# Batch 1's k' transposed by DMA with its projection one slot sooner, and the last output tile in three parts

## The chip, the cores and the metric

The kernel runs on one core of a Trainium2 chip. The metric is the time of one execution in microseconds (us), as the device reports it; lower is better. "Span" is the time from the first to the last instruction in a profiled execution; the reported time of the same execution is 1.7 to 1.8 us longer.

## The reference

Two parts, one behind the other. Linformer attention projects k and v along the sequence, so that scores are taken against 64 projected rows. Then comes a feed-forward network (FFN) with a quick GELU.

```python
k_proj = einsum('ks,bhsd->bhkd', E, k)          # E, F: 64 x 1024
v_proj = einsum('ks,bhsd->bhkd', F, v)          # 8 batches, 8 heads, 1024 rows, 64 wide
scores = (1/8) * q @ k_proj^T
attn   = softmax(scores)
x      = (attn @ v_proj)  -> 8192 tokens x 512
h      = x @ w_in                               # 512 x 2048
out    = (h * sigmoid(1.702 h)) @ w_out         # 2048 x 512
```

## The kernel before

The FFN works on 16 blocks of 512 tokens. In a block, 16 groups of four matmuls ("slots" 0 to 15) make `h`; then eight parts of eight matmuls (slots O = 16 and up) make the output, two parts for each of four output tiles. Attention for later blocks is put into those slots with `at(block, slot, work)`, so that TensorE never stands still. The parts that matter here:

```python
ps_f = ctx.enter_context(tc.tile_pool(name="ps_f", bufs=4, space=PSUM))   # f_tile: four buffers in rotation
...
def proj(b):                                   # k' and v' of batch b, 16 matmuls
    def go():
        kvps[b] = f_tile([P, H, D])
        ...
def k_tr(b, k_b, p0):                          # k' transposed on TensorE
    t_ps = f_tile([P, n, KP], BF16)
    for p in range(n):
        nc.tensor.transpose(t_ps[:, p, :], ..., ident[:KP, :KP])
    nc.vector.tensor_copy(kts[b % 2][:, p0:p0 + n, :], t_ps)
...
def kv_out(b):
    def go():
        ps = kvps.pop(b)
        k_b = att.tile([KP, H, D], BF16, name="k_b")
        nc.vector.tensor_copy(k_b, ps[LO])     # "the cast of k'"
        if b > 1:                              # batches 2 to 7: k' transposed by DMA
            nc.sync.dma_start_transpose(out=kts[b % 2], in_=k_b.rearrange("k h d -> k (h d)"))
        v_out(b, ps)
        kbs[b] = k_b
    return go
...
# the last output tile: two halves of 256 columns
for i, cp in enumerate((nc.scalar.copy, nc.vector.tensor_copy)):
    ms = slice(i * DM // 2, (i + 1) * DM // 2)
    l_ps = f_tile([P, DM // 2])
    for fc in range(FC):
        nc.tensor.matmul(l_ps, gts[j][:, fc, n * P:(n + 1) * P], w_out_sb[:, fc, ms], ...)
    cp(osb[j][:, n, ms], l_ps)
    nc.sync.dma_start(out=ov[:, c * JB + n, ms], in_=osb[j][:, n, ms])
...
at(1, 10, proj(1))
at(1, 11, kv_out(1))
at(1, 13, lambda: k_tr(1, kbs[1], 0))
at(1, 1, q_dma(1, 0, JB), q_dma(1, JB, JB))    # q of batch 1 transposed by DMA, same queue
for u in range(2):
    at(1, O, scores(2, u, None, u > 0))        # the first scores of batch 1: need k' of batch 1
...
load(j // NB2 + 2)                             # GpSimd's loads, two batches ahead: k, q, v for batch 2
```

There is one `k_sb` and one `v_sb` buffer (`bufs=1`). The load of batch b+1's k can therefore start only when the projection of batch b has read its own k. The projection sets free a 1 MB load.

The softmax here doesn't subtract the row's maximum and nothing guards it: scores larger than these inputs give would overflow.

Of the kernel before, what the change touches and what calls it, by code (L numbers as in the profile page):

```python
# [17 lines left out]
def kernel(ctx, tc, q, k, v, E, F,  # L18
                                                     moe_w_in, moe_w_out, out):
    nc = tc.nc  # L20
    B, H, S, D = q.shape
    KP, _ = E.shape
    DM, DFF = moe_w_in.shape
    P = 128
# [87 lines left out]
    kts = [consts.tile([P, HP, KP], BF16, name=f"kt{i}") for i in range(2)]  # L112
# [25 lines left out]
    def f_tile(shape, dt=F32):  # L138
        return ps_f.tile(shape, dt, name="f_ps")

    def warm(n):
        w_ps = ps_x.tile([P, TB], F32, name="x_ps")
        for _ in range(n):
            nc.tensor.matmul(w_ps, zeros[:, :P], zeros, start=True, stop=True)  # L144
# [6 lines left out]
    for i, cp in enumerate((nc.vector.tensor_copy, nc.scalar.copy)):  # L151
        t_ps = f_tile([P, J // 2, 2 * KP], BF16)
# [10 lines left out]
    def eft(j, cols=slice(0, 2 * KP)):  # L163
        return efts[j // (J // 2)][:, j % (J // 2), cols]


    kvps, kbs, qT, expT, xT, rbc, rdens = {}, {}, {}, {}, {}, {}, {}

    def proj(b):
        def go():  # L170
            kvps[b] = f_tile([P, H, D])
            for j in range(J):
                for e, r in enumerate((LO, HI)):
                    nc.tensor.matmul(kvps[b][r], eft(j, slice(e * KP, (e + 1) * KP)),  # L174
                                     (kt, vt)[e][b][:, :, j, :],
                                     start=(j == 0), stop=(j == J - 1))
        return go

    def proj0(e, h0, n):
        ps = f_tile([P, n, D])  # L180
        for j in range(J):
            nc.tensor.matmul(ps, ffs[:, j].rearrange("s i k -> s (i k)") if e else eft(j), (kt, vt)[e][0][:, h0:h0 + n, j, :],
                             start=(j == 0), stop=(j == J - 1))
        return ps

    def k_piece(h0, n):
        k_ps = proj0(0, h0, n)
        k_b = att.tile([KP, n, D], BF16, name=f"k0_b{h0}", bufs=1)
        nc.vector.tensor_copy(k_b, k_ps[LO])
        warm(2)  # L190
        k_tr(0, k_b, h0 // 2)

    def k_tr(b, k_b, p0):
        n = k_b.shape[1] // 2
        t_ps = f_tile([P, n, KP], BF16)
        for p in range(n):
            nc.tensor.transpose(t_ps[:, p, :], k_b[:, 2 * p:2 * p + 2, :].rearrange("k t d -> k (t d)"),
                                ident[:KP, :KP])
        nc.vector.tensor_copy(kts[b % 2][:, p0:p0 + n, :], t_ps)

    def vx_of(b, p):
        if b == 1:
# [13 lines left out]
    def v_out(b, v_ps):  # L216
        vv = v_ps[HI].rearrange("k (u x) d -> k u x d", x=4)
        for r, xs_ in ((LO, X_LO), (HI, X_HI)):
            if b == 1:
                vx = vx1[r, :, :D].rearrange("k (u x) d -> k u x d", x=4)  # L220
                nc.vector.tensor_copy(vx[:, :, xs_], vv[:, :, xs_])
            nc.vector.tensor_copy(vqs[b % 2][r].rearrange("k (u e) d -> k u e d", e=2), vv[:, :, xs_, :])

    def kv_out(b):
        def go():
            ps = kvps.pop(b)
            k_b = att.tile([KP, H, D], BF16, name="k_b")
            nc.vector.tensor_copy(k_b, ps[LO])  # L228
            if b > 1:
                nc.sync.dma_start_transpose(out=kts[b % 2], in_=k_b.rearrange("k h d -> k (h d)"))  # L230
            v_out(b, ps)
            kbs[b] = k_b
        return go

    q0s = [[consts.tile([P, 2, 2, P], BF16, name=f"q0T{g}{u}") for u in range(2)] for g in range(2)]
# [21 lines left out]
    def q_dma(b, j0=0, n=J):  # L257
        def go():
            if j0 == 0:
                qT[b] = att.tile([P, J, HP, P], BF16, name="qT")  # L260
            nc.sync.dma_start_transpose(out=qT[b][:, j0:j0 + n].rearrange("r j p s -> r (j p) s"),
                                        in_=qt[b][:, j0:j0 + n].rearrange("s j h d -> s (j h d)"))
        return go
# [102 lines left out]
    def x_tr(h, p, half):  # L366
        def go():
            x_sb = xs.pop((h, p, half)).rearrange("s (i t) d -> s i (t d)", i=2)
            n_ps = ps_x.tile([P, 2, P], BF16, name="x_ps")
            for i in range(2):  # L370
                nc.tensor.transpose(n_ps[:, i, :], x_sb[:, i, :], ident)  # L371
            cp = nc.scalar.copy if (h, half) == (0, 0) else nc.vector.tensor_copy
            cp(x_of(h)[:, p, half * TB // 2:(half + 1) * TB // 2], n_ps.rearrange("r i s -> r (i s)"))
        return go
# [22 lines left out]
    def ffn2(j, n, fcs):  # L397
        b, c = divmod(j, NB2)
        ov = out[b * S:(b + 1) * S, :].rearrange("(p j) m -> p j m", j=J)
        if j not in osb:  # L400
            osb[j] = work.tile([P, JB, DM], F32, name="o_sb")
        if j == NBLK - 1 and n == JB - 1:

            if fcs.start == 0:
                for i, cp in enumerate((nc.scalar.copy, nc.vector.tensor_copy)):
                    ms = slice(i * DM // 2, (i + 1) * DM // 2)
                    l_ps = f_tile([P, DM // 2])
                    for fc in range(FC):
                        nc.tensor.matmul(l_ps, gts[j][:, fc, n * P:(n + 1) * P], w_out_sb[:, fc, ms],  # L409
                                         start=(fc == 0), stop=(fc == FC - 1))  # L410
                    cp(osb[j][:, n, ms], l_ps)  # L411
                    nc.sync.dma_start(out=ov[:, c * JB + n, ms], in_=osb[j][:, n, ms])
            return
        if fcs.start == 0:
            o_ps[n] = f_tile([P, DM])
        for fc in fcs:
            nc.tensor.matmul(o_ps[n], gts[j][:, fc, n * P:(n + 1) * P], w_out_sb[:, fc, :],  # L417
                             start=(fc == 0), stop=(fc == FC - 1))
        if fcs.stop == FC:
            nc.scalar.copy(osb[j][:, n, :], o_ps.pop(n))  # L420
            if j == NBLK - 1:
                nc.sync.dma_start(out=ov[:, c * JB + n, :], in_=osb[j][:, n, :])
            elif n == JB - 1:
                nc.sync.dma_start(out=ov[:, c * JB:(c + 1) * JB, :], in_=osb[j])
# [3 lines left out]
    def at(j, slot, *fs):  # L428
        fill.setdefault((j, slot), []).extend(fs)
# [3 lines left out]
    for h0, n in ((0, 4), (4, 2), (6, 2)):  # L433
        k_piece(h0, n)
# [35 lines left out]
    for p in range(HP):  # L470
        at(0, Q + (2, 4, 6, 7)[p], tok(1, p, 0), tok(1, p, 1))
        at(0, Q + (4, 6, 7, 8)[p], x_tr(1, p, 0), x_tr(1, p, 1))
    at(1, 10, proj(1))
    at(1, 11, kv_out(1))
    at(1, 13, lambda: k_tr(1, kbs[1], 0))
    at(1, 1, q_dma(1, 0, JB), q_dma(1, JB, JB))
    for u in range(2):
        at(1, O, scores(2, u, None, u > 0))
# [38 lines left out]
    for j in range(NBLK):  # L517
        if j % NB2 == 0 and j // NB2 + 2 < B:
            load(j // NB2 + 2)
        for i, (half, fc) in enumerate(order if j == 0 else [(None, fc) for fc in range(FC)]):  # L520
            ffn1(j, fc, slice(0, TB) if half is None else slice(half * TB // 2, (half + 1) * TB // 2))
            filled(j, i)
        parts = [(n, range(8 * g, 8 * g + 8)) for n in range(JB) for g in range(2)]
        if j == 0:
            parts[:4] = [(n, fcs) for fcs in (range(8), range(8, 12), range(12, FC)) for n in range(2)]
        for s, (n, fcs) in enumerate(parts):
            ffn2(j, n, fcs)
            filled(j, (Q if j == 0 else O) + s)
# [31 lines left out]
```

## Time and profile before

| | before |
|---|---|
| median of the first three runs | 511.01 us (510.7 to 511.32) |
| span of the profiled execution | 509.6 us |
| TensorE busy, share of the chain | 99%, 93% |
| from block 1's first FFN matmul (55.19) to the first scores of batch 1 (73.10) | 17.91 us |
| from block 1's first FFN matmul to the first matmul of the last tile (502.43): the "stretch" | 447.24 us |
| from there to the end: the "tail" | 7.21 us |

The last three rows are differences of start times in the trace. The stretch measures what the change does in the middle, the tail what it does at the end, and neither contains the start of the kernel, which varies from one execution to the next.

### The profile page before, as it was taken

The page shows a single profiled execution, that of the slowest core. Times are in us where ns is not written, and L with a number is a line of the kernel's source. Part 1 is how long each engine was busy: PE and PEld are TensorE (multiplying, and loading weights), DVE is VectorE, ACT ScalarE, POOL GpSimd, SP SyncE. Part 2 cuts the span into 40 slices and gives each one's busy share as a digit, 9 for nine tenths or more (in the row PEclk, how much of TensorE's full clock was granted, in tenths as well). Part 3 has the DMA queues.
Part 4 walks back from the last instruction along what each step waited for, and adds up shares of the span by engine and source line. Part 5 has one row for each costly group of instructions (what it writes and reads, how often), then busy time and mean ns, then how long its engine had stood idle before and what let it go on. Part 6 is the DMA issues. An engine that isn't in the chain of part 4 may idle for free.

```text
span 509.6 us, 7212 instructions
## 1 busy us (share of the span) xinstructions
PE 503.0 (99%) x3082; PEld 232.2 (46%) x3082; DVE 158.2 (31%) x219; ACT 263.8 (52%) x443; POOL 78.0 (15%) x97
## 2 busy tenths in 40 slices
PE   8899999999999999999999999999999999999997
PEld 4585445444444444444444444444444444444444
DVE  4523114607151623216161330616223161611000
ACT  1675563664637365572746537374563737253451
POOL 7442051510600510041000510000000000000000
PEclk9999999999999999999999999999999999999999
DMA  9999999999999997598938969090603205050202
GB/s 167 197 202 207 210 140 170 228 207 137 179 195 266 116 213 125 141 150 98 228 54 223 103 117 228 23 227 1 171 1 85 83 20 147 1 167 1 82 1 82
DMA packets 125305, 68.71 MB, mean 135 GB/s; under 512 B 92325, under 2 KB 116133, under 8 KB 123353
## 3 DMA queue, kind: packets, MB, share of 16 engines
q0 software_dynamic: 84400, 29.37, 51.2%
q1 hardware_dynamic: 40792, 38.62, 29.9%
q8 instruction: 24, 0.39, 0.3%
q10 hardware_dynamic: 80, 0.26, 0.2%
q14 instruction: 9, 0.07, 0.0%
HBM read 72.88 MB, written 16.99 MB: 176 GB/s over the span
## 4 chain that ended last, share of the span: by engine, by line
PE 93%; DMA 4%; POOL 1%; issue 0%; DVE 0%; ACT 0%; POOLq 0%
PE f_ps L417 43%; PE f_ps L385 43%; PE f_ps L174 3%; DMA w_in_sb<-in_moe_w_in_dram 2%; DMA v_sb<-in_v_dram 2%; PE f_ps L271 2%; PE x_ps L271 1%; PE x_ps L309 1%; POOL k_sb L57 0%; PE x_ps L356 0%; PE x_ps L371 0%; PE f_ps L409 0%; PE f_ps L253 0%; POOL q_even L57 0%; POOL v_sb L57 0%
## 5 line engine op out<-in xcount | busy, mean ns | idle before, releaser
L417 PE MATMUL f_ps<-w_out_sb,gT 128*128 128x512 bf16 x1008 | 226.7, 379 | 0.0
L385 PE MATMUL f_ps<-xT,w_in_sb 128*128 128x512 bf16 (+1 forms) x1088 | 225.9, 367 | 0.7 <-ACT gT L388 0.3
L388 ACT ACTIVATE gT<-f_ps 128x512 bf16<-128x512 f32 (+1 forms) x270 | 151.7, 574 | 59.1 <-PE f_ps L385 57.8
L385 PEld LDWEIGHTS <-w_in_sb 128*128 128x128 bf16 x1088 | 105.5, 98 | 116.1 <-DMA w_in_sb<-in_moe_w_in_dram 0.9
L417 PEld LDWEIGHTS <-gT 128*128 128x128 bf16 x1008 | 95.9, 98 | 121.6 <-issue 11.8
L420 ACT COPY o_sb<-f_ps 128x512 f32<-128x512 f32 x63 | 36.9, 586 | 130.7 <-PE f_ps L417 121.0
L344 DVE TENSOR_TENSOR xT<-x_ps,rbc 128x512 bf16<-128x512 f32 x52 | 33.3, 684 | 217.5 <-PE x_ps L271 120.4
L312 DVE RECIPROCAL rden<-x_ps 128x512 f32<-128x512 f32 x26 | 85.3, 3322 | 10.4 <-PE x_ps L309 10.3
L70 POOL DMA_DIRECT2D q_sb<-in_q_dram x48 | 42.0, 905 | 151.1 <-DMA qT<-q_sb 122.3
L290 ACT ACTIVATE expT<-f_ps 128x512 bf16<-128x512 f32 (+1 forms) x58 | 30.1, 573 | 29.9 <-PE f_ps L271 29.9
L290 ACT ACT_TABLE_LOAD x13 | 16.7, 1283 | 4.7 <-PE f_ps L271 4.5
L294 ACT ACT_TABLE_LOAD x14 | 18.0, 1283 | 0.2
L228 DVE CAST k_b<-f_ps 64x512 bf16<-64x512 f32 x7 | 4.8, 683 | 38.8 <-PE f_ps L174 38.8
L57 POOL DMA_DIRECT2D k_sb<-in_k_dram x10 | 8.5, 854 | 52.4 <-PE f_ps L174 50.8
L174 PE MATMUL f_ps<-k_sb,eft 128*64 128x512 bf16 x56 | 13.4, 382 | 0.0
L174 PE MATMUL f_ps<-v_sb,eft 128*64 128x512 bf16 x56 | 13.4, 382 | 0.0
L144 PE MATMUL x_ps<-zeros 128*128 128x512 bf16 x34 | 11.7, 469 | 1.2 <-DVE zeros L115 1.2
L411 DVE COPY o_sb<-f_ps 128x256 f32<-128x256 f32 x1 | 0.4, 424 | 38.6 <-issue 38.6
L271 PE MATMUL f_ps<-qT,kt 64*32 64x512 bf16 x208 | 10.6, 386 | 0.0
L271 PE MATMUL x_ps<-expT,vq 64*32 64x512 bf16 x208 | 10.2, 378 | 0.0
L363 DVE TENSOR_TENSOR x_sb<-x_ps,rd 128x256 bf16<-128x256 f32 x22 | 9.3, 424 | 0.8
L57 POOL DMA_DIRECT2D v_sb<-in_v_dram x10 | 8.4, 840 | 7.2 <-DMA q_sb<-in_q_dram 5.2
(71 smaller groups left out, 124.5 us busy)
## 6 DMA issues: line engine op xcount, KB each, us to landing
out_dram<-o_sb SPq DMA_DIRECT2D x15, 1024.0 KB
rbc<-rdr SPq DMA_DIRECT2D x26, 512.0 KB
k_sb<-in_k_dram POOLq DMA_DIRECT2D x7, 1024.0 KB, 13.7
v_sb<-in_v_dram POOLq DMA_DIRECT2D x7, 1024.0 KB, 18.1
q_sb<-in_q_dram POOLq DMA_DIRECT2D x48, 128.0 KB, 6.2
w_in_sb<-in_moe_w_in_dram POOLq DMA_DIRECT2D x8, 256.0 KB, 12.2
w_out_sb<-in_moe_w_out_dram POOLq DMA_DIRECT2D x4, 512.0 KB, 14.7
q_even<-in_q_dram POOLq DMA_DIRECT2D x8, 128.0 KB, 10.9
```

What stands on the lines that cost most here:

```text
L57: nc.gpsimd.dma_start(out=dst[b][:, h:h + n, js:js + jn], in_=sv[:, h:h + n, js:js + jn])
L70: nc.gpsimd.dma_start(out=qt[b][:, j], in_=qv[:, j])
L174: nc.tensor.matmul(kvps[b][r], eft(j, slice(e * KP, (e + 1) * KP)), (kt, vt)[e][b][:, :, j, :], start=(j == 0), stop=(j == J - 1))
L271: nc.tensor.matmul(outs[i][r.start + c:r.start + c + 32], lhsTs[i][ri, c:c + 32], rhss[i][ri], start=True, stop=True)
L290: nc.scalar.activation(expT[h][:, 2 * u + i, ts], s_ps[i], AF.Exp, scale=scale)
L294: nc.scalar.preload_act_table(AF.Gelu_apprx_sigmoid)
L312: nc.vector.reciprocal(rden[:, e, :], d_ps[e])
L344: nc.vector.tensor_tensor(x_of(h)[:, 2 * u + i, :], n_ps[i], rbc[h][:, 2 * u + i, :], op=ALU.mult)
L385: nc.tensor.matmul(h_ps, w_in_sb[:, kc, fc * P:(fc + 1) * P], xT[j][:, kc, ts], start=(kc == 0), stop=(kc == KC - 1))
L388: nc.scalar.activation(gts[j][:, fc, ts], h_ps, AF.Gelu_apprx_sigmoid)
L417: nc.tensor.matmul(o_ps[n], gts[j][:, fc, n * P:(n + 1) * P], w_out_sb[:, fc, :], start=(fc == 0), stop=(fc == FC - 1))
L420: nc.scalar.copy(osb[j][:, n, :], o_ps.pop(n))
```

## The change

The intent is to take k' of batch 1 off TensorE, the engine that bounds the kernel, as is already done for batches 2 to 7; and to shorten the end by making the last copy and the last transfer small. The projection moves from slot 10 to slot 9, and the cast from 11 to 9, to give the DMA transpose time. The core of the diff:

```diff
@@ in kv_out @@
-            if b > 1:
-                nc.sync.dma_start_transpose(out=kts[b % 2], in_=k_b.rearrange("k h d -> k (h d)"))
+            nc.sync.dma_start_transpose(out=kts[b % 2], in_=k_b.rearrange("k h d -> k (h d)"))
             v_out(b, ps)
-            kbs[b] = k_b
...
-                for i, cp in enumerate((nc.scalar.copy, nc.vector.tensor_copy)):
-                    ms = slice(i * DM // 2, (i + 1) * DM // 2)
-                    l_ps = f_tile([P, DM // 2])
+                for m0, m, cp in ((0, 2, nc.vector.tensor_copy), (2, 1, nc.vector.tensor_copy), (3, 1, nc.scalar.copy)):
+                    ms = slice(m0 * DM // 4, (m0 + m) * DM // 4)
+                    l_ps = f_tile([P, m * DM // 4])
...
-    at(1, 10, proj(1))
-    at(1, 11, kv_out(1))
-    at(1, 13, lambda: k_tr(1, kbs[1], 0))
+    at(1, 9, proj(1), kv_out(1))
```

(`k_tr` loses its batch argument, and stays for batch 0.)

More of the change, by code (lines that the diff above doesn't have):

```diff
@@ L164, in eft @@
         return efts[j // (J // 2)][:, j % (J // 2), cols]
-    kvps, kbs, qT, expT, xT, rbc, rdens = {}, {}, {}, {}, {}, {}, {}
+    kvps, qT, expT, xT, rbc, rdens = {}, {}, {}, {}, {}, {}
     def proj(b):
@@ L190, in k_piece, with k_tr @@
         warm(2)
-        k_tr(0, k_b, h0 // 2)
-    def k_tr(b, k_b, p0):
+        k_tr(k_b, h0 // 2)
+    def k_tr(k_b, p0):
         n = k_b.shape[1] // 2
@@ L198, in k_tr @@
                                 ident[:KP, :KP])
-        nc.vector.tensor_copy(kts[b % 2][:, p0:p0 + n, :], t_ps)
+        nc.vector.tensor_copy(kts[0][:, p0:p0 + n, :], t_ps)
     def vx_of(b, p):
```

## The prediction

> **What bounds the kernel now.** I read the page's busy table and its chain first, then the groups, then the chain in order of time around the two edited places, then the timelines there.
>
> ```profile
> span 509.6 us, 7212 instructions
> ...
> PE 503.0 (99%) x3082; PEld 232.2 (46%) x3082; DVE 158.2 (31%) x219; ACT 263.8 (52%) x443; POOL 78.0 (15%) x97
> ...
> PE 93%; DMA 4%; POOL 1%; issue 0%; DVE 0%; ACT 0%; POOLq 0%
> ...
> L417 PE MATMUL f_ps<-w_out_sb,gT 128*128 128x512 bf16 x1008 | 226.7, 379 | 0.0
> ```
>
> TensorE is busy for 99% of the span and holds 93% of the chain; the groups of FFN matmuls show no idle time before them. DVE (31%) and ACT (52%) have room. So time can be gained only by taking instructions off TensorE, or in the tail after its last matmul. The granted clock is 0.999, so there is nothing to win there. The reported median (511.01) is 1.4 us above the span (509.6); I take that offset as fixed.
>
> First edited place, the chain in order of time (start, length, what):
>
> ```profile
> 64.85 1.85 PE f_ps L174 x16
> 66.70 2.70 PE f_ps L385 x12
> 69.39 0.22 PE f_ps L197 x4
> 69.61 1.83 PE f_ps L385 x8
> 71.45 1.73 PE f_ps L417 x8
> 73.17 0.34 PE f_ps L271 x8
> ```
>
> L174 is batch 1's projection, L197 the four transposes of k', L271 the scores of batch 1, which need k'. All pieces touch: nothing here waits. A plain pair of four-matmul groups is 8 x 0.216 = 1.73 us (the L417 piece); the pair right after the transposes takes 1.83. So the transposes cost 0.22 themselves and 0.10 in the group behind them.
>
> Second edited place, the tail in the timeline (start, length, engine):
>
> ```profile
> 502.43 3.66 PE L409 MATMUL f_ps<-w_out_sb,gT 128*128 128x256 bf16 x32
> ...
> 504.38 0.37 ACT L411 COPY o_sb<-f_ps 128x256 f32<-128x256 f32 x1 [1.16 <-PE f_ps L409]
> 504.78 2.19 SPq L412 DMA_DIRECT2D out_dram<-o_sb  x2
> 506.18 0.42 DVE L411 COPY o_sb<-f_ps 128x256 f32<-128x256 f32 x1 [38.63 <-issue]
> ```
>
> Matmuls end at 502.43 + 3.66 = 506.09; DVE copies from 506.18 to 506.61; the last output transfer is issued from about 506.64 (each of the two issues takes 0.33); the closing waits, in which the queue waited 1.3 us for that output, end at 509.6. All of this is on the end path.
>
> **What the Trainium skill says.** "TensorEngine Tiling (Array Packing)", Key Properties: changing the tiling mode drains TensorE. The trace agrees: after the projection (128*64 tiles) the next 12 FFN matmuls take 2.70 instead of 12 x 0.216 = 2.59, after the k' transposes (64*128) 1.83 instead of 1.73. So a 0.22 us group costs 0.32. "TensorE: Matmul & The Clock Gate", Back-to-back issue gap, gives about 81 ns per matmul of 128 columns in a real stream and 56 isolated, and 131 for 512. The trace does not agree with its stream figures: 512 columns take 216 ns (1.73 / 8). For 128 columns with new 128x128 weights each time, this kernel has runs of eight that start at 16.61 and are followed at 17.06: 0.45 / 8 = 56 ns. I use 56. "DMA: Bandwidth & Descriptors", Anatomy of one DMA, puts most of a transfer's fixed cost in the write receipt, so a smaller transfer keeps most of its cost; here the last one takes 1.8 us from its issue to the end of its wait, whereas its packets were busy for about 0.5 us of that. Its Specifications name 512 B as the least size at line rate; the new pieces are 128 x 4 B = 512 B a row, just at it, and no 512 B write is in this trace.
>
> **The change part by part.**
>
> (1) k' of batch 1 leaves TensorE: four 64x64 matmuls, with their weight loads, and one DVE copy (0.29 us, hidden) go. Off the end path: 0.22 + 0.10 = **0.32 us**.
>
> (2) The projection (1.85 us) moves one FFN group of four matmuls (0.86 us) earlier, and the cast of k' goes with it. That moves work along TensorE and costs nothing, if nothing waits. Three waits to check.
> - Inputs: v of batch 1 was issued at 31.06, and the POOL queue's wait for its landing ended at 53.8; the projection would start at 64.8 - 0.86 = 63.9. Ready.
> - The PSUM buffer: four f_ps buffers in rotation. The fourth allocation after the projection reuses its buffer. Before, that was the transposes; now it is the fourth FFN group after the projection, starting near 69.23 - 0.86 = 68.37. DVE frees the buffer 0.86 earlier than before, where its last copy was 68.61 + 0.42 = 69.03: at 68.17. It is 0.2 us early. No wait, though not by much.
> - k' itself: see (3).
>
> ```profile
> 66.77 0.68 DVE L228 CAST k_b<-f_ps 64x512 bf16<-64x512 f32 x1 [12.72 <-PE f_ps L174]
> ...
> 68.61 0.42 DVE L222 CAST vq<-f_ps 64x256 bf16<-64x256 f32 x1
> ```
>
> (3) One DMA transpose is added. The cast will end at 66.77 - 0.86 + 0.68 = 66.6, and the queue issues then: in front of it lie only the two q transposes, whose issue ended at 57.47 + 7.03 = 64.5 and whose packets end at about 66.8. The nearest precedent is batch 3's, also behind a q transpose:
>
> ```profile
> 121.50 4.96 SPq L261 DMA_TRANSPOSE qT<-q_sb  x1
> 126.51 1.24 SPq L230 DMA_TRANSPOSE kt<-k_b  x1
> ```
>
> Its packets were over about 2.1 us after the issue (in the stretch 126.4 to 128.8 the DMA share falls to 0 at 128.5). The worst I found, at 361.65 behind two broadcasts, took some 3.2 us. So k' lands between 68.7 and 69.9; the scores will ask for it at 73.1 - 0.32 = 72.8. Slack **3 to 4 us**: hidden. The loads of batch 2, released by the projection, also start 0.86 us sooner; TensorE did not wait for them before.
>
> (4) The last output tile: 16 x 256 columns + 16 x 256 columns becomes 16 x 256 + 16 x 128 + 16 x 128. The second half took 16 x 0.109 (3.39 / 31 from the group); 32 x 0.056 = 1.79 against 16 x 0.109 = 1.74: the last matmul starts 0.09 us later. But a 128-column matmul is recorded with 0.219 against 0.273 us, so its result is there only 0.04 later, near 506.13.
>
> (5) The last copy. ACT starts 0.04 after the result where DVE took 0.09 (first half: 504.38 against 504.34; DVE 506.18 against 506.09). ACT's copies:
>
> ```profile
> L420 ACT COPY o_sb<-f_ps x63: 585/585/620, 46.0 to 502.6; 128x512 f32<-128x512 f32 x63
> ...
> L411 ACT COPY o_sb<-f_ps x1: 373/373/373, 504.4 to 504.4; 128x256 f32<-128x256 f32 x1
> L411 DVE COPY o_sb<-f_ps x1: 424/424/424, 506.2 to 506.2; 128x256 f32<-128x256 f32 x1
> ```
>
> (585 - 373) / 256 = 0.83 ns a column, so 128 columns are about 0.27 us (estimate from these). The copy ends at 506.13 + 0.04 + 0.27 = 506.44 against 506.61: **0.17 us** sooner. DVE's middle copy ends near 505.7, its transfer is issued by 506.1, so the queue is free.
>
> (6) The last transfer halves. Its packets of 1 KB took 48 ns and those of 2 KB 87, each engine with eight; on that line 512 B is 29 ns (estimate). 8 x (48 - 29) = **0.15 us** sooner.
>
> (7) The closing waits go through the transfers' semaphores one after another, about 0.06 us each. The last transfer's semaphore was followed by five more; with two transfers added to the rotation, three follow it. **0.12 us**.
>
> Sum: 0.32 + 0.17 + 0.15 + 0.12 = 0.76 us. 511.01 - 0.76 = 510.25 us, that is 0.15% faster.
>
> **The rivals.**
> - *The transpose becomes a wait.* If its landing took over 6.2 us, the scores would stand still for the rest. For: the DMA engines are nearly always busy in this stretch, and the first packets of batch 2's loads arrive with it. Against: 2.1 to 3.2 us in the two precedents. A landing at 9 us would give about 513.
> - *128-column matmuls cost 81 ns, as the skill's stream figure has it.* Then (4) costs 32 x 0.025 = 0.8 us, and the time is about 511.0. For: all 32 change weights. Against: the measured runs of eight at 56 ns.
> - *The PSUM buffer binds.* If DVE runs 0.3 us late, the fourth group waits 0.1 us and (1) shrinks to 0.2: 510.4.
> - *The transfer's end is all fixed cost* (receipt, not packets), or 512 B writes are slower than their line: (6) vanishes and 510.4 stands.
> - *Something later takes it back*: a transfer that is needed at a fixed time. Against: the chain after 27.95 us has no DMA in it at all.
>
> **The range and the chances.** The three runs before spread from 510.7 to 511.32, as much as the whole gain; the median of the next three can lie 0.3 off. Small failures of (4) to (7) would raise it by 0.1 to 0.3, a full wait in (3) is unlikely (5%). I put 510.25, range 509.7 to 510.9. A change over 2% is 10 us, far beyond any term here.
>
> **What would show it.** In the changed profile: no L197-like transposes between the projection and the scores of batch 1, and a chain there without a DMA or a gap (right), or with a DMA of k' before the scores (wrong). Batch 1's cast of k' at 65.9, its transpose issued at 66.6. In the tail 32 matmuls of 128 columns 56 ns apart; ACT's last copy at 0.27 us; the end 0.3 to 0.45 us nearer to the last matmul's start than before. The span should be near 508.9. The prediction is wrong if the span shrinks by less than 0.3 or by more than 1.2 us, or if the scores at 72.8 wait.

## The result

The changed kernel took 511.02 us (median of four runs, 510.73 to 511.23), the kernel before 511.09 in the same rounds. The ratio is 0.9999 with a 95% interval of 0.9982 to 1.0016. A ratio is the mean time of one kernel's fast runs over the mean of the other's in the same rounds, so it is not quite the ratio of the medians. The prediction of 510.25 (509.7 to 510.9) missed.

The page of the changed kernel, in the lines that answer to those shown of before (line numbers are two lower behind the edit: L415, L383 and L269 are the former L417, L385 and L271):

```profile
span 509.2 us, 7242 instructions
...
PE 502.8 (99%) x3094; PEld 232.5 (46%) x3094; DVE 158.4 (31%) x219; ACT 263.7 (52%) x443; POOL 78.0 (15%) x97
...
PE 92%; DMA 6%; POOL 1%; issue 0%; DVE 0%; ACT 0%; POOLq 0%
...
L269 PE MATMUL f_ps<-qT,kt 64*32 64x512 bf16 x208 | 10.7, 386 | 0.4 <-DMA kt<-k_b 0.4
```

A share of the chain has gone from TensorE to DMA, and the scores, which had waited for nothing, show 0.4 us of idle time that a transfer into `kt` ended. The chain in order of time shows where (start, length, what):

```profile
63.98 1.89 PE f_ps L174 x16
65.87 0.02 issue
65.90 0.69 DVE k_b L228
66.59 0.02 issue
66.61 6.59 DMA kt<-k_b
73.20 0.04 issue
73.25 0.41 PE f_ps L269 x8
```

Up to 66.61 all is as predicted: the cast at 65.90, the transpose issued at 66.61. But it lands **6.59 us** later, not 2.1 to 3.2. The scores start at 73.25, 0.15 us later than before, where 72.8 was forecast.

The tail in the timeline of the changed kernel:

```profile
502.58 3.70 PE L407 MATMUL f_ps<-w_out_sb,gT 128*128 128x256 bf16 x48
...
504.58 0.42 DVE L409 COPY o_sb<-f_ps 128x256 f32<-128x256 f32 x1 [36.88 <-issue]
505.03 1.90 SPq L410 DMA_DIRECT2D out_dram<-o_sb  x3
505.42 0.29 DVE L409 COPY o_sb<-f_ps 128x128 f32<-128x128 f32 x1 [0.41 <-PE f_ps L407]
506.31 0.27 ACT L409 COPY o_sb<-f_ps 128x128 f32<-128x128 f32 x1 [2.95 <-PE f_ps L407]
```

The last copy takes 0.27 us and ends at 506.58, 4.00 us behind the tile's first matmul; before it was 4.17 (506.61 - 502.43). The whole tail is 6.67 us against 7.21: **0.54 us gained**. So in this profile the middle loses 0.15 and the tail gains 0.54. The net gain is 0.4 us, the timed rounds show none, and the forecast was 0.76.

Two questions follow: why does k' land so late, and where is the 0.4 us?

**A look back at the kernel before.** My precedents for the landing were the k' transposes issued at 126.51 and 361.65. There are four more, at 92.74, 181, 241 and 301. Before the prediction I had asked for DMA views of 92 to 104 us and of 181 to 184.5 us, and I drew on neither. This is the timeline of the kernel before around 301 (start, length, engine; POOL is GpSimd, SPq the queue that issues the transposes), and then the DMA view of the stretch from 305 to 307 us (packets by size; then packets, MB and engine share of each queue, q0 being GpSimd's loads, q1 the queue of the transposes):

```profile
301.01 0.88 POOL L57 DMA_DIRECT2D k_sb<-in_k_dram  x1 [10.12 <-PE f_ps L174]
...
301.50 1.19 SPq L230 DMA_TRANSPOSE kt<-k_b  x1
```

```profile
DMA packets 503, 0.34 MB, mean 168 GB/s; under 512 B 233, under 2 KB 503, under 8 KB 503
## 3 DMA queue, kind: packets, MB, share of 16 engines
q0 software_dynamic: 270, 0.28, 93.3%
q1 hardware_dynamic: 233, 0.06, 22.5%
```

From 3.5 to 5.5 us after the issue, the 256-byte packets of that transpose are still moving beside the load of the next k. Nobody waits for them there, because the scores of that batch come at 318.6, 17 us later, so no view of waits names them. Around the issue at 126.51 the DMA view (124 to 129 us) has no packet of GpSimd's queue at all, and GpSimd's last load of the whole kernel was issued at 301.88, long before 361.65. Both of my precedents were the ones without a load.

Not all of the delay at 301.5 is the load's. Packets of 2 KB, of a broadcast ahead in the same queue, move until 304.6, as they do at 361.65 until 364.6. But from there the 256-byte packets of k' take 3.1 us beside the load (304.8 to 307.8), and 1.1 us where there is none (363.8 to 364.9).

The transpose at 92.74 is nearest to the changed one: its load was issued at 92.25, half a microsecond ahead. The DMA views that I already had, of 96 to 98, 98 to 100 and 100 to 104 us, show its packets late:

```profile
92.74 2.09 SPq L230 DMA_TRANSPOSE kt<-k_b  x1
...
q1 hardware_dynamic: 1, 0.00, 0.0%
...
q1 hardware_dynamic: 104, 0.03, 15.5%
...
q1 hardware_dynamic: 184, 0.04, 9.4%
```

The 256-byte packets run from 98.1 to 101.6, so they end 8.9 us after the issue (here an output of 1 MB also stood ahead in the queue, until 96.1). "The worst I found, at 361.65" was thus not the worst on view.

That gives a theory: **the load that the projection itself sets free delays the transpose.** The rival is the place in the queue: k' stands behind the q transposes of batch 1, whose packets end at 66.9.

### The profile page after: what moved, and what is told of

Read it like the earlier page. It is cut to its first block, busy times and chain, and to the rows that moved or that the text cites. A ratio compares the mean times of both kernels' runs of the same rounds, so it can differ in the third digit from the quotient of the medians.

```text
span 509.2 us, 7242 instructions
## 1 busy us (share of the span) xinstructions
PE 502.8 (99%) x3094; PEld 232.5 (46%) x3094; DVE 158.4 (31%) x219; ACT 263.7 (52%) x443; POOL 78.0 (15%) x97
## 4 chain that ended last, share of the span: by engine, by line
PE 92%; DMA 6%; POOL 1%; issue 0%; DVE 0%; ACT 0%; POOLq 0%
PE f_ps L415 43%; PE f_ps L383 42%; PE f_ps L174 3%; DMA w_in_sb<-in_moe_w_in_dram 2%; DMA v_sb<-in_v_dram 2%; PE f_ps L269 2%; PE x_ps L269 1%; DMA kt<-k_b 1%; PE f_ps L407 1%; PE x_ps L307 1%; POOL k_sb L57 0%; PE x_ps L354 0%; PE x_ps L369 0%; PE f_ps L251 0%; POOL q_even L57 0%
## 5 line engine op out<-in xcount | busy, mean ns | idle before, releaser
L415 PE MATMUL f_ps<-w_out_sb,gT 128*128 128x512 bf16 x1008 | 226.7, 379 | 0.0
L383 PE MATMUL f_ps<-xT,w_in_sb 128*128 128x512 bf16 (+1 forms) x1088 | 225.7, 367 | 0.6 <-ACT gT L386 0.3
L383 PEld LDWEIGHTS <-w_in_sb 128*128 128x128 bf16 x1088 | 105.6, 98 | 116.2 <-DMA w_in_sb<-in_moe_w_in_dram 0.9
L415 PEld LDWEIGHTS <-gT 128*128 128x128 bf16 x1008 | 95.9, 98 | 121.5 <-issue 11.8
L269 PE MATMUL f_ps<-qT,kt 64*32 64x512 bf16 x208 | 10.7, 386 | 0.4 <-DMA kt<-k_b 0.4
L269 PE MATMUL x_ps<-expT,vq 64*32 64x512 bf16 x208 | 10.2, 378 | 0.0
L359 DVE RECIPROCAL rd<-x_ps 128x4 f32<-128x4 f32 x22 | 3.8, 174 | 17.8 <-PE x_ps L354 17.8
```

The costliest lines, as they stand in the source:

```text
L269: nc.tensor.matmul(outs[i][r.start + c:r.start + c + 32], lhsTs[i][ri, c:c + 32], rhss[i][ri], start=True, stop=True)
L383: nc.tensor.matmul(h_ps, w_in_sb[:, kc, fc * P:(fc + 1) * P], xT[j][:, kc, ts], start=(kc == 0), stop=(kc == KC - 1))
L415: nc.tensor.matmul(o_ps[n], gts[j][:, fc, n * P:(n + 1) * P], w_out_sb[:, fc, :], start=(fc == 0), stop=(fc == FC - 1))
```

## The experiments

All kernels gave the right result. "Changed" below is the changed kernel; edits are against it unless said otherwise.

### The two parts alone, and the changed kernel again

`after_again` is the changed kernel without an edit.

> The changed kernel unaltered, to settle what the four rounds left open: 0.9999 with an interval of 0.9982 to 1.0016. The two profiles say that the tail is 0.55 us shorter and that the scores of batch 1 start 0.15 us later, 0.40 us in all, ratio 0.9992. If the time is really the same (1.0000 within 0.0003), something outside those two places takes the 0.4 us back. In the profile: k' again lands 6 to 7 us after its transpose was issued at 66.6, and the first scores of batch 1 start at 73.2 to 73.3.

Ratio 1.0004 (0.9988 to 1.002). Scores 17.92 us behind block 1's first matmul, stretch 447.26, tail 6.68. The profile again shows a gain in the tail and none in the middle.

`tail_only` is the kernel before with this edit alone:

```diff
-                for i, cp in enumerate((nc.scalar.copy, nc.vector.tensor_copy)):
+                for m0, m, cp in ((0, 2, nc.vector.tensor_copy), (2, 1, nc.vector.tensor_copy), (3, 1, nc.scalar.copy)):
   (and the two lines of ms and l_ps)
```

> The kernel before with only the last output tile in three parts (256, 128, 128 columns). If the tail gains by itself: scores of batch 1 at 73.10 as before, the last matmul's start 0.09 us later than before, the span 0.45 to 0.55 us shorter than before (near 509.1), ratio 0.9990. The closing waits keep one more transfer than before, so 4 of them follow the last landing, and 0.06 us of the gain is lost. If the tail's gain depends on the rest: less than 0.2 us.

Stretch 447.24, exactly as before; tail 6.71, that is 0.50 shorter. The ratio was 0.9998 (0.9986 to 1.0011). The span of 509.8 missed the expectation, because this execution's block 1 began 0.7 us later than in the profile of before (55.89 against 55.19): whole times of single executions are no measure here. In the profile the tail's gain stands by itself; the timed ratio cannot tell the expected 0.9990 from 1.

`kt_only` is the changed kernel with the last tile in two halves, as before (the diff above, reversed).

> The kernel before with only batch 1's k' by DMA and its projection one slot sooner, the last tile in two halves. If the late landing eats the gain: scores of batch 1 at 73.2 to 73.3, all of TensorE 0.15 us later than before to its last matmul, ratio 1.0003 (0.06 us may come back from one closing wait fewer). If the prediction's 0.32 us were right: scores at 72.8 and ratio 0.9994.

```profile
63.49 1.89 PE f_ps L174 x16
...
66.11 6.70 DMA kt<-k_b
72.85 0.41 PE f_ps L269 x8
```

A landing of 6.70 us again. The scores come 18.16 us behind block 1's first matmul, 0.25 later than before, and the stretch is 447.50. The ratio was 1.0011 (0.9993 to 1.0029). So in its profile the first part of the change, alone, loses 0.25 us; the timed ratio, whose interval holds 1, does not show it.

### Earlier still

```diff
-    at(1, 9, proj(1), kv_out(1))
+    at(1, 7, proj(1), kv_out(1))
```

> The changed kernel with batch 1's projections two slots sooner still (slot 7 in place of 9), so that k' is cast near 64.2+0.7 = 64.9 and its transpose issued then. Theory: the landing is late because batch 2's load of k, which the same projection sets free, shares the 16 DMA engines with it; the load moves with the projection, so k' lands again some 6.6 us after the issue, near 71.5, before the scores need it at 72.8, and they start at 72.8: 0.47 us better than the changed kernel, ratio to before 0.9983. Rival: k' has to wait for the q transposes in front of it in the same queue, which end at 66.9 whatever its issue; then it lands no earlier than in the changed kernel, near 73.2, and nothing is gained.

```profile
62.07 1.89 PE f_ps L174 x16
63.99 0.68 DVE k_b L228
64.70 0.43 DVE vx L221
65.24 9.98 DMA kt<-k_b
75.27 0.62 PE f_ps L269 x5
```

Both expectations fail. Issued 1.4 us sooner, k' lands **2.0 us later**, and the scores wait 2.6 us. The ratio is 1.003 (1.0006 to 1.0054), with the whole interval above 1. The six runs are not alike. Three took 513.7 to 515.2 us, two of these with a granted clock of 0.996 and 0.997; three took 511.4 to 511.8 at a clock of 1.000, near the 511.28 of before. The trace is of one of the long ones (514.43), so its 9.98 us need not hold for all. The timeline says what became different:

```profile
64.22 0.88 POOL L57 DMA_DIRECT2D k_sb<-in_k_dram  x1 [9.22 <-PE f_ps L174]
...
65.24 2.27 SPq L229 DMA_TRANSPOSE kt<-k_b  x1
```

The load follows the projection at once, at 64.22. The transpose could not be issued when its cast was done (64.7), because the queue was still issuing the q transposes. The load stood ahead by 1.0 us in place of 0.5, while q transposes were still under way: 681 small packets move between 67 and 68 us, where the changed kernel has none. So "earlier" was no cure here: the load moves along, and the rival's fixed time (73.2 whatever the issue) is wrong as well. A mixture of both remained possible, so the next step was to take the load away.

### The load held back

In `gate_k`, GpSimd copies one element of the transposed k' before it issues batch 2's loads: that of k, and the seven of q that follow it. The q transposes of batch 1 still stand in front of k'.

```diff
+    def load_gated():
+        nc.gpsimd.tensor_copy(gate, kts[1][:, 0, :1])
+        load(2)
-    at(1, 9, proj(1), kv_out(1))
+    at(1, 9, proj(1), kv_out(1), load_gated)
```

(The loop's own call of `load(2)` falls away.)

> The changed kernel with batch 2's loads held back until k' of batch 1 has landed (GpSimd copies one element of it before it issues the load). The q transposes still stand in front of k' in the queue. Theory, the load of k is what delays it: k' lands 2 to 2.5 us after its issue at 66.6, the scores of batch 1 start at 72.8 without a wait. Rival, the queue behind the q transposes or a landing that is slow by itself: 6 to 7 us as before, scores at 73.2. By the way the loads start near 68.8 in place of 66.1, so v of batch 2 may come too late for its projection near 90: a stall of 0 to 2 us there would follow from the hold, not from k'.

GpSimd's copy started at 69.56, 2.34 us after the transpose's issue at 67.22: that is the landing. The scores came 17.59 us behind block 1's first matmul, 0.32 sooner than before, with no wait. The theory holds and the rival falls: the q transposes are still in front, and k' is fast. (The gate holds back all of batch 2's loads, so the runs do not separate the load of k from the issuing of q's behind it.) The price was as foretold: the loads began at 70.04 (1.2 us later than reckoned, half of it because this execution's block 1 began 0.6 us later), v of batch 2 came too late, and TensorE stood 2.0 us. The chain shows it:

```profile
81.70 0.22 PE x_ps L369 x4
82.14 10.56 DMA v_sb<-in_v_dram
92.74 1.89 PE f_ps L174 x15
```

The one look took 513.52 us. As a kernel that is worse; as a test it is clean.

In `gate_cast` GpSimd waits only for the cast (`kbs[1][:, 0, :1]`, with `kbs[b] = k_b` kept in `kv_out`). The load is then issued behind the transpose instead of ahead of it.

> The changed kernel with batch 2's loads held back only until k' of batch 1 is cast (GpSimd copies one element of the cast first), so that load and transpose are issued in the opposite order: the transpose at 66.6, the load some 0.2 us after it, 0.65 us later than in the changed kernel. If the load delays k' only when it stands ahead: landing 2 to 3 us after the issue, scores at 72.8, the middle of the kernel 0.32 us shorter than before, ratio 0.9983. If sharing the DMA engines is what counts, whatever the order: landing after 4.5 to 6.5 us, and a wait of 0 to 0.4 us stays.

The timeline, and the DMA view of the stretch from 67.2 to 68.8 us:

```profile
66.61 1.17 SPq L229 DMA_TRANSPOSE kt<-k_b  x1
...
66.64 0.18 POOL L475 COPY gate<-k_b 64x1 bf16<-64x1 bf16 x1 [11.74 <-DVE k_b L228]
...
67.13 0.88 POOL L57 DMA_DIRECT2D k_sb<-in_k_dram  x1 [0.31 <-PE f_ps L384]
```

```profile
DMA packets 293, 0.07 MB, mean 44 GB/s; under 512 B 289, under 2 KB 293, under 8 KB 293
## 3 DMA queue, kind: packets, MB, share of 16 engines
q1 hardware_dynamic: 289, 0.07, 23.4%
q0 software_dynamic: 4, 0.00, 1.9%
```

The packets of k' are through between 67.2 and 68.8, before the load's data move, about 2.2 us after the issue. The scores come at 17.59, without a wait. The ratio is **0.9982** (0.9967 to 0.9996) against an expected 0.9983. The load was issued 1.0 us later than in the changed kernel, not 0.65 as expected, and a part of the gain was paid for it: in the projection of batch 2 the first matmul on v starts 0.25 us behind the first on k (89.96 and 89.71; before, both started at 90.04). The stretch was 447.12, 0.12 and not 0.32 shorter than before, and the tail 6.63: 0.70 us by the profile, a ratio of 0.9986, which the timed interval holds. The expected ratio was met, but not by the expected sum.

Set beside this, the changed kernel in the same place. The timeline, then the DMA views of 67 to 69 us and of 70.5 to 71.5 us:

```profile
66.12 0.87 POOL L57 DMA_DIRECT2D k_sb<-in_k_dram  x1 [11.46 <-PE f_ps L174]
66.61 1.17 SPq L229 DMA_TRANSPOSE kt<-k_b  x1
```

```profile
DMA packets 60, 0.06 MB, mean 31 GB/s; under 512 B 0, under 2 KB 60, under 8 KB 60
## 3 DMA queue, kind: packets, MB, share of 16 engines
q0 software_dynamic: 60, 0.06, 29.6%
```

```profile
## 3 DMA queue, kind: packets, MB, share of 16 engines
q0 software_dynamic: 153, 0.16, 94.1%
q1 hardware_dynamic: 147, 0.04, 29.5%
```

The delay has two parts. From 67 to 69 not one small packet moves, although the engines are busy for only 30% of the time, and although with the load behind they were moving within 67.2 to 68.8: k' is not outrun for bandwidth there, it has not begun. Later both queues run side by side, 147 packets of one against 153 of the other in a microsecond, and the 256 data packets of k', which took 0.5 us when alone (67.8 to 68.3 in `gate_cast`), take 2.9 (69.3 to 72.2). The first part is worth 1.5 us (the first packet moves 2.7 us after the issue, against 1.2), the second 2.4. That second part agrees with the Trainium skill, "DMA: Bandwidth & Descriptors", Queues, rings and completion order: each engine takes turns between the queues with work, packet by packet. No run here shows what holds the first part.

### The wait taken away instead of the landing

`late_scores` leaves the transpose and the load alone, and asks for k' later.

```diff
+    at(1, O, lambda: nc.scalar.preload_act_table(AF.Exp))
     for u in range(2):
-        at(1, O, scores(2, u, None, u > 0))
+        at(1, O + 1, scores(2, u, None, u > 0))
```

> The changed kernel with the scores of batch 1's first half one output part (1.73 us) later, and ScalarE's table for Exp loaded ahead of them, so that k' may land 1.7 us later without a wait. k' still lands 6 to 7 us after its issue, near 73.2; the scores start near 74.5 and wait for nothing. If the wait is all that took the gain: the stretch from the first FFN matmul of block 1 to the last output tile is 0.32 us shorter than before and the tail 0.54 shorter, ratio 0.9983 and a span near 508.8 if the kernel starts as before. If something else stands behind it (values for the next tile, a PSUM buffer): a new wait near 76 to 78.

```profile
63.75 1.85 PE f_ps L174 x16
65.60 5.29 PE f_ps L383 x24
70.89 3.45 PE f_ps L415 x16
74.34 0.34 PE f_ps L269 x8
```

The chain no longer leaves TensorE. The stretch is **446.92 us, 0.32 below before**, to the hundredth what the prediction gave to the removed transposes. The tail is 6.67. The ratio is **0.9983** (0.9967 to 0.9998), as expected, and no new wait appeared. Beside the changed kernel:

> The changed kernel once more, beside the version with late scores in the same call. Theory: its gain in the tail (0.54 us) is partly or wholly taken back by a wait for k' whose length changes from one execution to the next (0.33 to 0.5 us in three profiles so far, against the 0.32 us that the removed transposes give). Ratio to before 0.9990 to 1.0005; the stretch from block 1's first matmul to the last tile between 447.2 and 447.8 us (447.24 before).

> The version with late scores once more: its stretch to the last tile again 446.92 us, its tail 6.67, no wait for k'; ratio to before 0.9980 to 0.9988, and lower than that of the changed kernel in the same call by about 0.0010. Rival, that 0.9983 was a lucky draw of noisy runs: ratios of the two within 0.0003 of each other.

Changed: 1.0003 (0.999 to 1.0016), stretch 447.44, tail 6.67. Late scores: **0.9982** (0.9969 to 0.9995), median 510.35 us, stretch 446.92, tail 6.65. Late scores were faster than the kernel before in both calls, with both intervals below 1. In the second call each of their five runs (509.91 to 510.78) was below each of the six of the changed kernel (510.93 to 511.75). The two ratios differ by 0.0021, where about 0.0010 was expected.

### Is the wait longer than the profiles show?

Open was that late scores time where their profile says, while the changed kernel, 0.4 us ahead by its profiles, times level. More looks:

> One more look at the changed kernel, for how much the wait changes between executions: k' lands 6 to 8 us after its issue, scores of batch 1 between 17.9 and 18.5 us after block 1's first matmul (17.91 before; 17.59 if there were no wait).

> As the look before it: the scores of batch 1 17.9 to 18.5 us after block 1's first matmul. If all looks lie within 0.1 us of 18.0, the wait does not change from run to run, and the spread of the times comes from elsewhere (the start of the kernel, before block 1).

> If the wait for k' has a long tail, some of these looks show the scores of batch 1 more than 18.3 us after block 1's first matmul (17.89 to 18.11 in five looks so far); if all stay within that band, the wait does not explain the level timing.

> As the look before it: over 18.3 us for a long wait, 17.9 to 18.1 for the usual one.

> As the look before it: over 18.3 us for a long wait, 17.9 to 18.1 for the usual one.

> The kernel before: scores of batch 1 again 17.91 us after block 1's first matmul, 447.24 us from there to the last tile, tail 7.21 us. Its start, up to block 1's first matmul, is 54.7 to 55.9 us as in the other looks; if that is so in both kernels, the start is where the spread of the times comes from.

Distances from block 1's first FFN matmul, in us (the wait is the distance to the scores less 17.59, which is what `gate_k` and `gate_cast` show without one):

| execution | block 1 starts at | to the scores | wait for k' | stretch | tail |
|---|---|---|---|---|---|
| before, two looks | 55.19, 55.41 | 17.91, 17.91 | none | 447.24, 447.24 | 7.21, 7.21 |
| changed, first profile | 55.18 | 18.06 | 0.47 | 447.39 | 6.67 |
| after_again | 55.04 | 17.92 | 0.33 | 447.26 | 6.68 |
| after_r3 | 55.60 | 18.11 | 0.52 | 447.44 | 6.67 |
| after_look2 | 55.12 | 17.89 | 0.30 | 447.22 | 6.67 |
| after_look3 | 55.50 | 18.07 | 0.48 | 447.40 | 6.67 |
| after_look4 | 54.78 | 18.13 | 0.54 | 447.46 | 6.67 |
| after_look5 | 55.58 | 18.05 | 0.46 | 447.38 | 6.67 |
| after_look6 | 54.67 | 18.28 | 0.69 | 447.61 | 6.67 |

The wait is the only one of these that changes between executions inside the kernel, by 0.4 us, and no look passed the 18.3 that I had set as a sign of a long wait, though the last, at 18.28, came close. On the mean of the eight, the stretch is 447.40, 0.16 longer than before, and the tail 0.54 shorter: 0.38 us net, a ratio of 0.9993. That lies inside all three intervals of the timed rounds. The start of the kernel, which neither part of the change touches, moves by 0.9 us in this table. So the profiles say 0.4 us faster, the rounds say 0.9999, 1.0004 and 1.0003 with intervals of 0.0013 to 0.0017 either way, and I cannot tell from these runs whether the executions of which no trace was kept wait longer or the rounds were merely noisy. That stays open; it is a matter of under 0.1%.

## Why the prediction was wrong, point by point

- *What bounds the kernel:* right. TensorE stayed at 99%, and every tenth gained or lost came from its order of work or from the tail.
- *Step (1), 0.32 us for the transposes:* right in size. The two versions without a wait have the scores at 17.59 against 17.91, and late scores keep the whole 0.32 to the last tile.
- *Step (2), no wait for the inputs or the PSUM buffer:* right. The chain of late scores has the FFN groups after the projection in one piece, 24 matmuls in 5.29 us. The PSUM buffer's margin of 0.2 us was enough.
- *Step (3), "k' lands between 68.7 and 69.9 ... Slack 3 to 4 us: hidden":* **this is the step that failed.** It landed at 73.2, 6.59 us after its issue where 2.1 to 3.2 were taken (6.4 to 6.8 in the eight profiles of the changed kernel), and the scores waited 0.3 to 0.7 us: more, on the mean, than step (1) had gained. The term was sized from precedents without a load beside them. The step named the load ("loads of batch 2 ... also start 0.86 us sooner") to ask whether TensorE waits for it; the rival named its packets beside the transpose and was set aside on the strength of the two precedents. The one at 92.74, behind its own load, was left out. `gate_k` and `gate_cast` land in 2.2 to 2.3 us once the load stands behind. The figure of the prediction was thus true of a transpose without the load, and the rival called "The transpose becomes a wait", with its threshold of 6.2 us and its 5%, was what came.
- *Steps (4) and (5), the third part and the copy:* right. The last matmul starts 3.48 us behind the tile's first (3.39 before): 0.09 later. Runs of 128 columns start 56 ns apart. The copy took 0.265 us against an estimate of 0.27, and ended 0.17 sooner.
- *Steps (6) and (7), the last transfer and the closing waits:* right in kind, a little small. From the last issue to the end it was 3.01 us and is 2.65, 0.36 less, where 0.15 + 0.12 = 0.27 was forecast. In the trace the 512-byte packets took 28 ns each (estimate 29), and the last of them ended 0.17 sooner after the issue; three closing waits in place of five gave 0.12; 0.07 is in the rest, between the last packet and the wait's end, and I did not look for its cause. The remark in the prediction that most of a transfer's fixed cost is the write receipt does not come out of this trace: in the kernel before, the last transfer's first packet moves 0.83 us after the issue, the packets take 0.52 us, and the wait for them ends 0.45 us after the last. (The section cited is about transfers that GpSimd issues; this one is SyncE's.)
- *The sum:* 0.32 + 0.44 = 0.76 was forecast. Measured in the profiles: -0.16 + 0.54 = 0.38; without the wait: 0.32 + 0.54 = 0.86, and timed twice at 0.9983 and 0.9982, about 0.9 us. The offset of 1.4 us between time and span, with which the prediction reckoned a span of 508.9, set a median of three runs against one other execution; within one execution it is 1.7 to 1.8.

## What to carry to other kernels

When an operation is moved to DMA, ask what else the same event sets free, and take its landing time from a precedent with that traffic beside it, even one that nobody waits for. Moving the producer earlier did not help here, because the competing load is tied to the same producer; asking for the result later did, and so did making the load come behind. A change of a few tenths of a microsecond in a 511 us kernel is read from distances inside profiles, and only confirmed by whole times.

## What the Trainium skill lacked or had wrong

- "DMA: Bandwidth & Descriptors": I found nothing in it on a small transfer of a hardware queue that is issued 0.5 us behind a 1 MB load of GpSimd's queue. Taking turns explains a slower flow (147 packets beside 153), not that none of the transfer's packets moves until 69 us while the engines are only 30% busy. The landing took 6.4 to 6.8 us behind the load, 10.0 with the load 1.0 us ahead and q transposes still under way, and 2.2 to 2.3 ahead of the load or without it.
- "TensorE: Matmul & The Clock Gate", Back-to-back issue gap: its figures for a real stream, about 81 ns at 128 columns and 131 at 512, are not met here. 32 matmuls of 128 columns, each with new weights, started 56 ns apart, and 512 columns take 216. These are the values that the section gives for an isolated gap.
- The same page, What's actually happening, has the clock fall after an idle window of about 3.4 us. In the version with slot 7 less was enough: TensorE stood still from 72.66, the granted clock was 0.50 from 74.86, 2.2 us later, to 78.28 (`--windows 75:78` shows the 0.50), and the whole standstill was 2.61 us. The length of the slow stretch, 3.4 us, and the half clock agree with the page. The stretch of that run grew by 1.4 us more than the later scores explain. The standstill of 2.0 us in `gate_k` left the clock at 1.00.
- No page that I read mentions that the closing waits of a kernel run through the transfers' semaphores one after another, about 0.06 us each, so that it matters how many follow the last transfer's own: five before, three after, 0.12 us.
